# Gelu's upper half by a type-changing DMA within SBUF in four of sixteen slices

## The chip, the cores and the metric

The kernel runs on one core of a Trainium2 chip. Its time is the device time of one execution in microseconds, as the median of several runs. The engines are named as the profile names them: PE (TensorE, with its weight loads as PEld), DVE (VectorE), ACT (ScalarE), POOL (GpSimd) and SP (SyncE).

## The reference

Two stages in float32. First, for each of 4 batches, 49 agents attend to 12480 keys, and then the 12480 queries attend to the agents (width 128). The result, 49920 rows of 128, goes through a feed-forward layer with 2048 hidden values and gelu in its sigmoid form.

```python
def sm(a, b):
    s = scale * (a @ b.transpose(0, 2, 1))
    e = np.exp(s - s.max(-1, keepdims=True))
    return e / (e.sum(-1, keepdims=True) + 1e-09)
agent_v = sm(agents, k) @ v
x = sm(q, agents) @ agent_v
h = x @ w_in
out = (h * (1.0 / (1.0 + np.exp(-1.702 * h)))) @ w_out
```

## The kernel before

**Two parts for a value.** The large matmuls take float32r operands. A value is held as an upper part (a copy to float32r) and a lower part (the value less the upper part). So gelu's result g has the tiles gh (upper) and gl = g - gh (lower), and the products with the weights are summed: upper by upper, lower by upper, upper by lower.

**Groups and slices.** The queries of a batch make 13 groups of 960, so there are 52 groups. Each group goes through the 2048 hidden values in 16 slices f of 128. `up` (L357) makes a slice: four matmuls into two PSUM tiles ph (L362, L364), two gelu on ACT into g (L369), then gh by ACT for even f (`HI_ON_ACT`, L371) or by DVE for odd f (L373), then gl by a subtraction on DVE (L374). `down` (L377) adds a slice to the output with six matmuls (L385): two with gh, two with gl, two with gh again. `down` of a slice is called LAG = 4 slices after its `up`. After a group's last `down`, `store` (L393) copies the sums out and SP stores them.

**Work beside the slices.** For each group, `split` (L165) prepares the queries two groups ahead on POOL: a small memset (L167) and two subtractions (L168, L169) into a tile `rest`, of which there are two. At f = 4 the scores of the next group's queries are made (`scores`, L172): PE writes two PSUM tiles ps_m in turn, of which there are only two, and DVE reduces each (L189); softmax and the transposes for the next group (L345, then L350 to L353 at f = 12) follow. In groups 0 to 5 of a batch (1 to 5 of the first), the keys of the next batch are worked on: two or three blocks in a group, each with a split on POOL at f = 0, 4 (and 8), and scores on PE at f = 5, 9 (and 13), which use the same two ps_m tiles. After the last of them `key_max` (L229) takes the maximum over the batch with two transposes on PE (L235, L241) and copies it to max_b (L242). Then POOL subtracts it from 13 blocks of scores (`key_shift`, L251), and in groups 6 to 11 ACT takes the exponents (L255), ACT and POOL make pairs of them (L260, L261), DVE makes pairs of the values (L267, L268), and PE and DVE add them up (L272, L287). The fourth batch has no such work beside it.

**What sets the order.** The program is written in the order of the loop at L540, and the tile framework's scheduler then places each engine's instructions in an order of its own. Each engine runs its instructions strictly in that order, and an instruction that waits holds back all behind it on its engine. A tile is reused only when its former contents have been read: g has 3 buffers, gh and gl 5 each.

Of the kernel before, what the change touches and what calls it, by code (L numbers as in the profile page):

```python
# [8 lines left out]
F32 = mybir.dt.float32  # L9
F32R = mybir.dt.float32r  # L10
# [7 lines left out]
P = 128  # L18
TB = 120
KB = 8  # L20
CH = 480
GT = 2 * CH
LAG = 4
# [11 lines left out]
K_AT = 5  # L35
FIRST_WORDS = (1, 3, 5, 7)
FIRST_UP = (0, 2, 4, 6)
HI_ON_ACT = (0, 2, 4, 6, 8, 10, 12, 14)
EPS = 1e-09

# [2 lines left out]
def kernel(  # L43
# [10 lines left out]
    nc = tc.nc  # L54
# [14 lines left out]
    gpool = ctx.enter_context(tc.tile_pool(name="gpool", bufs=3))  # L69
# [1 line left out]
    ps_o = ctx.enter_context(tc.tile_pool(name="ps_o", bufs=1, space=bass.MemoryType.PSUM))  # L71
    ps_m = ctx.enter_context(tc.tile_pool(name="ps_m", bufs=2, space=bass.MemoryType.PSUM))

# [1 line left out]
    ag_sb = const.tile([P, B, A], F32, name="ag_sb")  # L75
    nc.sync.dma_start(out=ag_sb, in_=agT)

    ident = const.tile([P, P], F32, name="ident")
    make_identity(nc, ident)
    # sel[k, m] = 1 where k and m name the same agent in either half  # L80
    sel = const.tile([P, P], F32, name="sel")
    nc.vector.memset(sel, 0.0)
    for c in range(2):
        nc.vector.tensor_add(
            out=sel[:, c * H : c * H + A], in0=ident[:, 0:A], in1=ident[:, H : H + A]
# [20 lines left out]
    part_max = const.tile([P, NKG, A], F32, name="part_max")  # L106
    max_b = const.tile([P, A], F32, name="max_b")

    # a float64's words, low then high, to the nearest float32; what is under
    # float32's range becomes zero and what is over it infinite  # L110
    def load_words(src, i):
        w = loads.tile([P, 512, 2], U32, name="words", tag="kv")
        nc.sync.dma_start(out=w.rearrange("p n w -> p (n w)"), in_=src[:, i * 1024 : (i + 1) * 1024])
        return w

    def to_float32(w, out=None):
        lo = w[:, :, 0]
        hi = w[:, :, 1]
        ts = nc.vector.tensor_scalar
        stt = nc.vector.scalar_tensor_tensor  # L120
        # 2 ** exponent, with the sign
        tmp = work.tile([P, 2, 512], U32, name="tmp", tag="rest")
        ex = tmp[:, 0].bitcast(I32)
        ts(out=ex.bitcast(U32), in0=hi, scalar1=20, scalar2=0x7FF, op0=ALU.logical_shift_right, op1=ALU.bitwise_and)
        ts(out=ex, in0=ex, scalar1=1023 - 127, scalar2=1023 + 128, op0=ALU.max, op1=ALU.min)
        ts(out=ex, in0=ex, scalar1=float(127 - 1023), scalar2=float(1 << 23), op0=ALU.add, op1=ALU.mult)
        stt(out=ex.bitcast(U32), in0=hi, scalar=0x80000000, in1=ex.bitcast(U32), op0=ALU.bitwise_and, op1=ALU.bitwise_or)
        # the mantissa's upper 45 bits as a whole number, rounded once
        m = work.tile([P, 512], U32, name="m21", tag="o")
        r = tmp[:, 1]  # L130
        ts(out=m, in0=hi, scalar1=0xFFFFF, scalar2=0x100000, op0=ALU.bitwise_and, op1=ALU.bitwise_or)
        ts(out=r, in0=lo, scalar1=8, scalar2=None, op0=ALU.logical_shift_right)
        stt(out=m.bitcast(F32), in0=m, scalar=float(1 << 24), in1=r, op0=ALU.mult, op1=ALU.add)
        if out is None:
            out = m.bitcast(F32)
        stt(out=out, in0=m.bitcast(F32), scalar=2.0**-44, in1=ex.bitcast(F32), op0=ALU.mult, op1=ALU.mult)
        return out

    def up_weights(i, w):
        to_float32(w, w_in_sb[:, i * 512 : (i + 1) * 512])  # L140

    def down_weights(i, w):
        s = slice(i * 4, (i + 1) * 4)
        wo = to_float32(w).rearrange("p (f c) -> p f c", c=C)
        nc.scalar.copy(out=wo_h[:, s, :], in_=wo)
        nc.vector.tensor_sub(out=wo_l[:, s, :], in0=wo, in1=wo_h[:, s, :].bitcast(F32))

    # ---- scores: a float32 is the sum of three bfloat16, and of the parts'
    # products all are summed but those under a float32 product's own rounding ----
    ag_part = const.tile([P, B, 3, A], BF16, name="ag_part")  # L150
    rest = ag_sb
    for i in range(3):
# [7 lines left out]
        w = t.bitcast(BF16).rearrange("p (n w) -> p n w", w=2)  # L160
        return w[:, :, 1], w[:, :, 0]

    # the upper half of a word is the first part; of what is left the upper
    # half is the second, and the third takes the place of the lower
    def split(t):  # L165
        r = work.tile([P, GT + PAD], F32, name="rest", tag="rest")
        nc.gpsimd.memset(t[:, GT:], 0.0)  # L167
        nc.gpsimd.tensor_sub(out=r, in0=t, in1=halves(t)[0])  # L168
        nc.gpsimd.tensor_sub(out=halves(r)[1], in0=r, in1=halves(r)[0])  # L169
        return halves(t)[0], halves(r)[0], halves(r)[1]  # L170
# [20 lines left out]
                nc.scalar.copy(out=o, in_=s[:, :, 0, :])  # L191
                nc.vector.tensor_add(out=o, in0=s[:, :, 1, :], in1=o)

# [1 line left out]
    def key_load(b, g):  # L195
        t = loads.tile([P, GT + PAD], F32, name="kt", tag="kv")
        nc.sync.dma_start(out=t[:, 0:GT], in_=kT[b, :, g * KB : (g + 1) * KB, :].rearrange("p j t -> p (j t)"))
        return t

    def first_key_scores(g, kt):  # L200
        # two batches' agents to a pass, as many columns as keep the clock up
        for c in range(2):
            ps = ps_m.tile([P, 512], F32, name="ps_m")
            for j in range(KB // 2):
                nc.tensor.matmul(  # L205
                    out=ps[:TB, j * 2 * A : (j + 1) * 2 * A],
                    lhsT=kt[:, c * KB // 2 + j, :],
                    rhs=ag_sb[:, 0:2, :].rearrange("p b a -> p (b a)"),
                    start=True,
                    stop=True,  # L210
                )
            s = ps[:TB, : KB * A].rearrange("p (j b a) -> p j b a", b=2, a=A)[:, :, 0, :]
            i = 2 * g + c
            nc.scalar.copy(out=score[:TB, i * KB // 2 : (i + 1) * KB // 2, :], in_=s)
        nc.vector.tensor_reduce(
            out=part_max[:TB, g, :],
            in_=score[:TB, g * KB : (g + 1) * KB, :].rearrange("p j a -> p a j"),
            axis=AX.X,
            op=ALU.max,
        )  # L220
# [87 lines left out]
            nc.vector.tensor_sub(out=wl[:, s], in0=pw, in1=wh[:, s].bitcast(F32))  # L308
        return wh, wl

# [1 line left out]
    def query_load(b, g):  # L312
        t = loads.tile([P, GT + PAD], F32, name="qt", tag="qt", bufs=2)
        nc.sync.dma_start(out=t[:, 0:GT], in_=qT[b, :, g * GT : (g + 1) * GT])
        return t
# [37 lines left out]
        nc.vector.tensor_sub(out=sb[0:H], in0=ps[H:P, :CH], in1=sb[H:P].bitcast(F32))  # L353
        return sa, sb

# [1 line left out]
    def up(f, wts, pairs):  # L357
        wh, wl = wts
        s = slice(f * P, (f + 1) * P)
        ph = [ps_h.tile([P, 512], F32, name="ph") for _ in range(2)]  # L360
        for c in range(2):
            nc.tensor.matmul(out=ph[c][:, :CH], lhsT=wh[:, s], rhs=pairs[c], start=True, stop=False)  # L362
        for c in range(2):
            nc.tensor.matmul(out=ph[c][:, :CH], lhsT=wl[:, s], rhs=pairs[c], start=False, stop=True)  # L364
        g = gpool.tile([P, 2, CH], F32, name="g")
        gh = gpool.tile([P, 2, CH], F32R, name="gh", bufs=LAG + 1)
        gl = gpool.tile([P, 2, CH], F32R, name="gl", bufs=LAG + 1)
        for c in range(2):
            nc.scalar.activation(out=g[:, c, :], in_=ph[c][:, :CH], func=AF.Gelu_apprx_sigmoid)  # L369
        if f in HI_ON_ACT:  # L370
            nc.scalar.copy(out=gh, in_=g)  # L371
        else:
            nc.vector.tensor_copy(out=gh, in_=g)  # L373
        nc.vector.tensor_sub(out=gl, in0=g, in1=gh.bitcast(F32))  # L374
        return gh, gl
# [21 lines left out]
            t0 = b * N + g * GT + c * CH  # L397
            nc.sync.dma_start(out=outT[:, t0 : t0 + CH], in_=o)

# [1 line left out]
    kts = {}  # L401
    vts = {}
    qts = {}
# [47 lines left out]
    def do_weights(b):  # L451
        wts[b] = agent_weights(accs.pop(b))

    # the first batch's keys and values have nothing to run beside, and lie
    # where the weights and the hidden values come to lie afterwards
    def first_keys():
        tags = [("g", 3), ("gh", LAG + 1), ("gl", LAG + 1)]
        tiles = []
        for tag, bufs in tags:
            tiles += [gpool.tile([P, KB, TB], F32, name="kt0", tag=tag, bufs=bufs) for _ in range(bufs)]  # L460
        return tiles[:NKG]

    for g, t in enumerate(first_keys()):
        nc.sync.dma_start(out=t, in_=kT[0, :, g * KB : (g + 1) * KB, :])
        kts[0, g] = t
# [10 lines left out]
    words = [load_words(w_out, i) for i in range(NF // 4)]  # L476
    for g in range(NKG):
        first_key_scores(g, kts.pop((0, g)))
# [5 lines left out]
    for g in range(NKG):  # L484
# [3 lines left out]
        for j in range(KB):  # L488
            nc.tensor.matmul(
                out=acc_ps[:A, : C + 1],  # L490
# [4 lines left out]
            )  # L495
        if g in FIRST_UP:
            up_weights(FIRST_UP.index(g), words_in[FIRST_UP.index(g)])
        if g == 6:
# [6 lines left out]
    do_weights(0)  # L505
    down_weights(0, words[0])

    # what is done for the next batch beside a group: in steps of the group's
    def beside(b, g):
        jobs = {}  # L510
        if b == 0 and g == 0:
# [25 lines left out]
    steps = B * NG * NF  # L537
    live = {}
    po = {}
    for t in range(steps + LAG):  # L540
        n, f = divmod(t, NF)
        if t < steps:
            b, g = divmod(n, NG)
# [19 lines left out]
        if t >= LAG:  # L563
            n, f = divmod(t - LAG, NF)
# [43 lines left out]
```

## Time and profile before

| | us |
|---|---|
| median of three runs | 2137.14 |
| the three runs | 2136.03, 2137.14, 2139.71 |
| the profiled execution (first to last instruction, its span) | 2139.6 |
| PE busy | 2083.2 (97%) |
| DVE busy | 1865.0 (87%) |
| ACT busy | 1611.9 (75%) |
| POOL busy | 519.8 (24%) |

The profile shows one execution. The page gives no time of it beside the span, so the span stands for its time. Rows of groups give the line, engine and operation, the tiles out<-in, the count, then busy time and mean length, and the idle time before with what ended it. Rows of the timeline begin with start and length in us; a bracket at the end is the engine's idle time before the row and what released it.

### The profile page before, as it was taken

The page shows a single profiled execution, that of the slowest core. Times are in us where ns is not written, and L with a number is a line of the kernel's source. Part 1 is how long each engine was busy: PE and PEld are TensorE (multiplying, and loading weights), DVE is VectorE, ACT ScalarE, POOL GpSimd, SP SyncE. Part 2 cuts the span into 40 slices and gives each one's busy share as a digit, 9 for nine tenths or more (in the row PEclk, how much of TensorE's full clock was granted, in tenths as well). Part 3 has the DMA queues.
Part 4 walks back from the last instruction along what each step waited for, and adds up shares of the span by engine and source line. Part 5 has one row for each costly group of instructions (what it writes and reads, how often), then busy time and mean ns, then how long its engine had stood idle before and what let it go on. Part 6 is the DMA issues. An engine that isn't in the chain of part 4 may idle for free.

```text
span 2139.6 us, 31613 instructions
## 1 busy us (share of the span) xinstructions
PE 2083.2 (97%) x12232; PEld 1777.1 (83%) x12232; DVE 1865.0 (87%) x2142; ACT 1611.9 (75%) x2590; POOL 519.8 (24%) x383
## 2 busy tenths in 40 slices
PE   8889989999999999999999999999999999999999
PEld 8678878888888887788888888778888888888887
DVE  6998998999889899899888899899898887888876
ACT  3567768977777776987777777798777877778786
POOL 4143445121123433421113342531110101001000
PEclk9999999999999999999999999999999999999999
DMA  9411221211111212112101212111100101010000
GB/s 265 119 48 49 65 73 38 61 48 50 38 38 47 66 47 56 47 56 56 56 20 47 63 49 56 55 51 53 47 19 19 38 19 38 19 38 20 25 14 19
DMA packets 49339, 108.57 MB, mean 51 GB/s; under 512 B 4252, under 2 KB 30172, under 8 KB 49188
## 3 DMA queue, kind: packets, MB, share of 16 engines
q1 hardware_dynamic: 49188, 106.55, 17.2%
q8 instruction: 96, 1.57, 0.3%
q14 instruction: 55, 0.45, 0.1%
HBM read 80.97 MB, written 25.56 MB: 50 GB/s over the span
## 4 chain that ended last, share of the span: by engine, by line
PE 81%; DVE 11%; issue 3%; ACT 3%; POOL 1%; DMA 1%; ACTq 0%; SPq 0%; DVEq 0%; POOLq 0%
PE po L385 43%; PE ph L362 15%; PE ph L364 14%; DVE gl L374 5%; DVE gh L373 2%; PE ps_m L272 1%; PE ps_m L182 1%; PE ps_m L184 1%; POOL score L251 1%; PE ps_m L205 1%; ACT g L369 1%; PE ps_m L345 1%; PE ps_m L306 1%; PE ps_m L183 1%; PE ps_m L185 1%
## 5 line engine op out<-in xcount | busy, mean ns | idle before, releaser
L374 DVE TENSOR_TENSOR gl<-g,gh 128x960 fp32r<-128x960 f32 x832 | 1034.4, 1258 | 189.4 <-ACT gh L371 174.3
L369 ACT ACTIVATE g<-ph 128x480 f32<-128x480 f32 x1664 | 855.2, 573 | 380.5 <-PE ph L364 265.7
L385 PE MATMUL po<-gl,wo_h 128*128 128x480 f32 x1664 | 501.9, 382 | 5.4 <-DVE gl L374 5.4
L385 PE MATMUL po<-gh,wo_h 128*128 128x480 f32 x1664 | 506.1, 383 | 0.7 <-ACT gh L371 0.7
L385 PE MATMUL po<-gh,wo_l 128*128 128x480 f32 x1664 | 501.6, 383 | 0.0
L371 ACT CAST gh<-g 128x960 fp32r<-128x960 f32 x416 | 416.0, 1000 | 10.9
L385 PEld LDWEIGHTS po<-gl,wo_h 128*128 128x128 f32 x1664 | 313.1, 189 | 60.0 <-DVE gl L374 9.2
L385 PEld LDWEIGHTS po<-gh,wo_h 128*128 128x128 f32 x1664 | 313.5, 189 | 53.2 <-ACT gh L371 1.1
L385 PEld LDWEIGHTS po<-gh,wo_l 128*128 128x128 f32 x1664 | 313.8, 189 | 49.9
L362 PE MATMUL ph<-sa,wh 128*128 128x480 f32 x832 | 332.5, 400 | 4.8 <-ACT g L369 4.8
L364 PE MATMUL ph<-sa,wl 128*128 128x480 f32 x832 | 319.3, 384 | 0.0
L362 PE MATMUL ph<-sb,wh 128*128 128x480 f32 x832 | 318.8, 383 | 0.0
L364 PE MATMUL ph<-sb,wl 128*128 128x480 f32 x832 | 316.6, 381 | 0.0
L373 DVE CAST gh<-g 128x960 fp32r<-128x960 f32 x416 | 298.6, 718 | 7.0 <-ACT g L369 6.6
L167 POOL MEMSET qt<- 128x8 f32 x52 | 5.7, 110 | 939.2 <-PE ps_m L185 472.0
L169 POOL TENSOR_TENSOR rest<-rest 128x968 bf16<-128x968 f32 x91 | 188.6, 2072 | 7.1
L362 PEld LDWEIGHTS ph<-sa,wh 128*128 128x128 f32 x832 | 157.7, 190 | 31.7 <-ACT g L369 10.8
L362 PEld LDWEIGHTS ph<-sb,wh 128*128 128x128 f32 x832 | 158.0, 190 | 26.6 <-ACT g L369 6.2
L364 PEld LDWEIGHTS ph<-sb,wl 128*128 128x128 f32 x832 | 156.9, 189 | 25.6 <-issue 1.0
L364 PEld LDWEIGHTS ph<-sa,wl 128*128 128x128 f32 x832 | 157.1, 189 | 24.7 <-issue 1.0
L168 POOL TENSOR_TENSOR rest<-qt 128x968 f32<-128x968 f32 x52 | 110.7, 2129 | 167.8 <-DMA qt<-qT 110.8
L184 PE MATMUL ps_m<-ag_part,rest 128*128 128x98 bf16 x728 | 110.2, 205 | 0.0
(103 smaller groups left out, 2077.8 us busy)
## 6 DMA issues: line engine op xcount, KB each, us to landing
kt<-kT SPq DMA_DIRECT2D x52, 480.0 KB, 3.6
qt<-qT SPq DMA_DIRECT2D x52, 480.0 KB, 3.8
vt<-v SPq DMA_DIRECT2D x52, 480.0 KB, 4.3
outT<-o SPq DMA_DIRECT2D x104, 240.0 KB, 2.2
words<-w_in SPq DMA_DIRECT2D x4, 512.0 KB, 10.9
words<-w_out SPq DMA_DIRECT2D x4, 512.0 KB, 8.2
ag_sb<-agT SPq DMA_DIRECT2D x1, 98.0 KB, 2.1
```

Source lines behind the costliest of these rows:

```text
L168: nc.gpsimd.tensor_sub(out=r, in0=t, in1=halves(t)[0])
L169: nc.gpsimd.tensor_sub(out=halves(r)[1], in0=r, in1=halves(r)[0])
L182: mm(out=o, lhsT=x0[:, t], rhs=a[:, 0 : 2 * A], start=True, stop=False)
L183: mm(out=o[:, A:], lhsT=x0[:, t], rhs=a[:, 2 * A :], start=False, stop=False)
L184: mm(out=o, lhsT=x1[:, t], rhs=a[:, 0 : 2 * A], start=False, stop=False)
L362: nc.tensor.matmul(out=ph[c][:, :CH], lhsT=wh[:, s], rhs=pairs[c], start=True, stop=False)
L364: nc.tensor.matmul(out=ph[c][:, :CH], lhsT=wl[:, s], rhs=pairs[c], start=False, stop=True)
L369: nc.scalar.activation(out=g[:, c, :], in_=ph[c][:, :CH], func=AF.Gelu_apprx_sigmoid)
L371: nc.scalar.copy(out=gh, in_=g)
L373: nc.vector.tensor_copy(out=gh, in_=g)
L374: nc.vector.tensor_sub(out=gl, in0=g, in1=gh.bitcast(F32))
L385: nc.tensor.matmul(out=po[c][:, :CH], lhsT=lhsT[:, f, :], rhs=rhs[:, c, :], start=(f == 0 and first), stop=(f == NF - 1 and last),)
```

## The change

In slices 1, 5, 9 and 13 of every group gh is no longer made by a DVE cast but by a DMA from g to gh, both in SBUF, issued on POOL's queue; it changes the type from float32 to float32r. DVE's subtraction for gl is still there and now waits for the DMA. g gets four buffers (three before), gl four (five before). The tiles in which the first batch's keys lie are the same buffers and are counted anew (still 13).

```diff
+HI_ON_DMA = (1, 5, 9, 13)
 HI_ON_ACT = (0, 2, 4, 6, 8, 10, 12, 14)
...
-        g = gpool.tile([P, 2, CH], F32, name="g")
+        g = gpool.tile([P, 2, CH], F32, name="g", bufs=LAG)
         gh = gpool.tile([P, 2, CH], F32R, name="gh", bufs=LAG + 1)
-        gl = gpool.tile([P, 2, CH], F32R, name="gl", bufs=LAG + 1)
+        gl = gpool.tile([P, 2, CH], F32R, name="gl", bufs=LAG)
         for c in range(2):
             nc.scalar.activation(out=g[:, c, :], in_=ph[c][:, :CH], func=AF.Gelu_apprx_sigmoid)
-        if f in HI_ON_ACT:
+        if f in HI_ON_DMA:
+            nc.gpsimd.dma_start(out=gh, in_=g)
+        elif f in HI_ON_ACT:
             nc.scalar.copy(out=gh, in_=g)
         else:
             nc.vector.tensor_copy(out=gh, in_=g)
...
-        tags = [("g", 3), ("gh", LAG + 1), ("gl", LAG + 1)]
+        tags = [("g", LAG), ("gh", LAG + 1), ("gl", LAG)]
```

In the changed kernel's own numbering, lines after the new constant stand one further down, and those after `up` three (L168 becomes L169, L373 becomes L376, L374 becomes L377, L385 becomes L388); the DMA is L372. The text uses the numbers of before unless an order of the changed kernel is shown.

On POOL, in a group with keys beside it (batch 1, its fifth group): rest is the tile of a split, kt and qt are a block of keys and the queries of a group. Before:

```order
L168 TENSOR_TENSOR rest_8383<-kt_8253 128x968
L169 TENSOR_TENSOR rest_8383<-rest_8383 128x968
L167 MEMSET kt_8714 128x8
L168 TENSOR_TENSOR rest_8596<-qt_8245 128x968
L169 TENSOR_TENSOR rest_8596<-rest_8596 128x968
L168 TENSOR_TENSOR rest_8710<-kt_8708 128x968
L169 TENSOR_TENSOR rest_8710<-rest_8710 128x968
```

And now:

```order
L169 TENSOR_TENSOR rest_8383<-kt_8253 128x968
L170 TENSOR_TENSOR rest_8383<-rest_8383 128x968
L168 MEMSET kt_8714 128x8
L169 TENSOR_TENSOR rest_8596<-qt_8245 128x968
L170 TENSOR_TENSOR rest_8596<-rest_8596 128x968
L372 DMA gh_8452<-g_8451 128x960
L169 TENSOR_TENSOR rest_8710<-kt_8708 128x968
L170 TENSOR_TENSOR rest_8710<-rest_8710 128x968
L372 DMA gh_8565<-g_8564 128x960
L372 DMA gh_8656<-g_8655 128x960
```

The DMA of slice 5 (gh_8452) stands behind two splits, that of slice 9 (gh_8565) behind the next group's first split, and that of slice 13 (gh_8656) behind nothing else.

On DVE, in the same group, from the subtraction of slice 1 (gl_8282) to the reduces of the query scores (sd from two ps_m tiles). Before:

```order
L373 CAST gh_8281<-g_8280 128x960
L374 TENSOR_TENSOR gl_8282<-g_8280,gh_8281 128x960
L374 TENSOR_TENSOR gl_8301<-g_8299,gh_8300 128x960
L373 CAST gh_8319<-g_8318 128x960
L374 TENSOR_TENSOR gl_8320<-g_8318,gh_8319 128x960
L189 TENSOR_REDUCE sd_8337<-ps_m_8338 120x196
L189 TENSOR_REDUCE sd_8337<-ps_m_8356 120x196
```

And now:

```order
L377 TENSOR_TENSOR gl_8282<-g_8280,gh_8281 128x960
L377 TENSOR_TENSOR gl_8301<-g_8299,gh_8300 128x960
L376 CAST gh_8319<-g_8318 128x960
L190 TENSOR_REDUCE sd_8337<-ps_m_8338 120x196
L377 TENSOR_TENSOR gl_8320<-g_8318,gh_8319 128x960
L190 TENSOR_REDUCE sd_8337<-ps_m_8356 120x196
```

The cast of slice 1 is gone; the subtraction that needs its DMA is still the first of these rows, and both reduces stand behind it.

On POOL again, where the batch's maximum has been taken (score is the scores, max_b the maximum, gh_9117 slice 13 of that group, gh_9215 slice 1 of the next). Before:

```order
L168 TENSOR_TENSOR rest_9470<-qt_9178 128x968
L169 TENSOR_TENSOR rest_9470<-rest_9470 128x968
L251 TENSOR_TENSOR score_105<-score_105,max_b_107 120x392 x13
L167 MEMSET qt_9606 128x8
L261 TENSOR_TENSOR e_pair0_90<-score_105,e_pair0_90 120x8x49
```

And now:

```order
L169 TENSOR_TENSOR rest_9470<-qt_9178 128x968
L170 TENSOR_TENSOR rest_9470<-rest_9470 128x968
L372 DMA gh_9026<-g_9025 128x960
L372 DMA gh_9117<-g_9116 128x960
L252 TENSOR_TENSOR score_105<-score_105,max_b_107 120x392 x13
L372 DMA gh_9215<-g_9214 128x960
```

The 13 shifts stand together as before, and slice 1's DMA stands behind all of them. On DVE the copy to max_b stood behind the subtraction of slice 14 and still does; the two steps before it (L237, L239) have moved ahead of slice 13's subtraction.

## Prediction

> **What bounds the kernel now.** I read the page's busy table first, then the windows, then the timeline of a group without side work, of one with keys beside it, and of the place where a batch's maximum is taken. The busy table:
>
> ```profile
> PE 2083.2 (97%) x12232; PEld 1777.1 (83%) x12232; DVE 1865.0 (87%) x2142; ACT 1611.9 (75%) x2590; POOL 519.8 (24%) x383
> ```
>
> The windows tell where PE is not full (columns: window, length, then busy us with counts for PE, PEld, DVE, ACT, POOL):
>
> ```profile
> 100.00:200.00 100.00, 91.97 (x622) 76.62 (x622) 94.81 (x106) 66.57 (x109) 41.91 (x27) 0.98 0.18 55
> 200.00:300.00 100.00, 95.38 (x651) 81.63 (x650) 91.57 (x98) 72.51 (x115) 38.54 (x24) 1.00 0.22 65
> 800.00:900.00 100.00, 94.06 (x536) 79.14 (x534) 92.09 (x101) 76.67 (x120) 41.05 (x27) 0.97 0.19 50
> 1000.00:1100.00 100.00, 100.00 (x538) 86.59 (x537) 87.69 (x102) 75.40 (x123) 11.81 (x12) 1.00 0.13 40
> 1300.00:1400.00 100.00, 95.57 (x623) 81.26 (x622) 93.24 (x102) 74.90 (x119) 53.11 (x33) 0.98 0.22 60
> 1400.00:1500.00 100.00, 97.79 (x522) 83.12 (x521) 93.14 (x107) 86.33 (x137) 17.31 (x13) 1.00 0.20 55
> 1900.00:2000.00 100.00, 100.00 (x543) 85.54 (x543) 81.35 (x92) 78.71 (x127) 7.75 (x7) 1.00 0.09 30
> ```
>
> PE is the bound almost everywhere; it has gaps only near the start and around 850 and 1350 us, where DVE is above 90%. All PE idle time is 2139.6 - 2083.2 = 56.4 us. So work taken from DVE can only win inside those few gaps, and anything that makes PE wait elsewhere is lost in full.
>
> A steady stretch shows what a slice costs and how early its values are:
>
> ```profile
> 1216.52 0.38 PE L362 MATMUL ph<-sa,wh 128*128 128x480 f32 x1
> 1217.37 1.03 ACT L369 ACTIVATE g<-ph 128x480 f32<-128x480 f32 x2
> 1218.43 0.66 DVE L373 CAST gh<-g 128x960 fp32r<-128x960 f32 x1
> 1218.70 0.38 PE L362 MATMUL ph<-sa,wh 128*128 128x480 f32 x1
> 1219.13 1.16 DVE L374 TENSOR_TENSOR gl<-g,gh 128x960 fp32r<-128x960 f32 x1
> ```
>
> A slice is 1218.70 - 1216.52 = 2.18 us of PE: ten matmuls 0.218 apart, four up and six down. g is ready 1.88 us after its slice starts (1217.37 + 1.03 = 1218.40). The slice's down matmuls run four slices later, behind that slice's four up matmuls (0.87 us), and take gh first and gl two matmuls (0.44 us) later. So gl is due 8.72 + 0.87 + 0.44 = 10.03 us after the slice starts, and of that 8.15 us lie after g. Less gl's own 1.16 us, a gh that takes up to 6.99 us is hidden, if nothing stands in its way.
>
> **The change, part by part.** Let W be the time from the moment POOL can issue the DMA until gh has landed.
>
> *Removed:* 4 of 8 casts of L373 in each of 52 groups.
>
> ```profile
> L373 DVE CAST gh<-g 128x960 fp32r<-128x960 f32 x416 | 298.6, 718 | 7.0 <-ACT g L369 6.6
> ACT g L369 <- DVE gl L374: 92.3, 74, 2.8
> ```
>
> 208 x 0.718 = 149 us of DVE, 2.87 us a group. Nearly all of it lies beside a full PE. It counts only in the groups with gaps: six near the start, and two each around 850 and 1350. Ten groups x 2.87 = 29 us at most, nothing at least. A fourth buffer of g also shortens ACT's waits for gl (92.3 us), which end in the same gaps. I take half: **-15 us**. gl goes from five buffers to four: gl(f+4) is written after up(f+4) and ACT's 1.03 us, when gl(f) has just been read (0.87 us after that up), so I cost it at nothing; a late PE would make DVE wait there, and nothing then waits for DVE.
>
> *Added: W.* The trace has no DMA from POOL, none within SBUF and none that changes a type. The nearest rows are loads of the same 480 KB in the same 128 rows, issued by SP:
>
> ```profile
> kt<-kT SPq DMA_DIRECT2D x52, 480.0 KB, 3.6
> qt<-qT SPq DMA_DIRECT2D x52, 480.0 KB, 3.8
> ```
>
> No reason makes POOL's faster, so 3.6 us is the low end. Writing the transfer's list in software and converting each value can each cost something; I bound both together by one more such transfer: 7.6 us. I take 3.8 + 1.0 = **4.8 us**, near the row it resembles. By the Trainium skill (DMA: Bandwidth & Descriptors, Anatomy of one DMA) a DMA from POOL takes about 2.0 us plus its bytes at 436 GB/s, 3.1 us here, and its table gives about 1 us to the first byte; an estimate from that page is W = 4.1 us and 2166 us in all by the sum below. No run shown here has such a DMA.
>
> In 35 of 52 groups 4.8 is under 6.99 and POOL is nearly idle: **0 us**.
>
> *Groups with keys (17: five, six and six).* Here DVE waits in its own order, and POOL's splits stand ahead of two of the four DMAs. One such group of before:
>
> ```profile
> 1296.59 0.66 DVE L373 CAST gh<-g 128x960 fp32r<-128x960 f32 x1
> 1302.84 1.04 DVE L189 TENSOR_REDUCE sd<-ps_m 120x196 f32<-120x392 f32 x2
> 1304.62 0.22 PE L182 MATMUL ps_m<-ag_part,kt 128*128 128x98 bf16 x1
> 1305.77 0.46 PE L362 MATMUL ph<-sa,wh 128*128 128x480 f32 x1
> 1306.74 2.67 POOL L168 TENSOR_TENSOR rest<-qt 128x968 f32<-128x968 f32 x1
> 1309.48 1.80 POOL L169 TENSOR_TENSOR rest<-rest 128x968 bf16<-128x968 f32 x1
> 1315.96 2.44 POOL L168 TENSOR_TENSOR rest<-kt 128x968 f32<-128x968 f32 x1 [4.67 <-PE ps_m L185]
> 1318.49 2.60 POOL L169 TENSOR_TENSOR rest<-rest 128x968 bf16<-128x968 f32 x1
> ```
>
> 1296.59 is slice 1's cast. Now DVE stands at gl(1) until 1296.59 + W, and behind it stand gl(2), gh(3), the first reduce of the query scores, gl(3) and the second: 3 x 1.16 for gl(1), gl(2) and gl(3), 0.66, 2 x 0.51 after the wait, so the second reduce is done at 1301.7 + W. The key scores at 1304.62 write those same two PSUM tiles, the second one 0.58 us in (half of their 1.15 us), at 1305.20. PE waits W - 3.45 = 1.35 us.
>
> Slice 5's DMA now stands behind two splits. The second ends at 1311.28; g(5) is there at 1305.77 + 1.88 = 1307.65. PE wants gl(5) at 1305.77 + 8.72 + 1.15 (slice 9's key scores) + 1.31 = 1316.95. From 1311.28 with W and 1.16 that holds to W = 4.5, and the 1.35 us that PE has just lost, less the 0.6 by which they delay the split, move it to 5.2: nothing at 4.8.
>
> Slice 9's DMA stands behind the next group's first split, which waits until slice 9's key scores let its buffer go and ends at 1321.09. Slice 9's up begins with it, near 1315.9; gl(9) is due 10.03 later, at 1325.95, and with 1.16 for gl the room is 3.7 us. PE waits W - 3.70 = 1.1 us.
>
> Together 2.45 us x 17 = **+42 us** (at W = 3.6: 3 us; at 7.6: 4.15 + 3.9 = 8.05, so 137 us).
>
> *The batch's maximum (three times).* POOL's order now has all 13 shifts ahead of slice 1's DMA of the next group.
>
> ```profile
> 844.72 1.94 ACT L369 ACTIVATE g<-ph 128x480 f32<-128x480 f32 x4
> 850.50 0.30 PE L241 MATMUL ps_m<-ident,mrow 49*120 49x49 f32 x1 [3.42 <-DVE mrow L239]
> 850.73 1.17 PE L385 MATMUL po<-gh,wo_h 128*128 128x480 f32 x2
> 853.30 0.60 PE L362 MATMUL ph<-sa,wh 128*128 128x480 f32 x1
> 853.70 0.60 PE L362 MATMUL ph<-sb,wh 128*128 128x480 f32 x1
> 856.22 0.60 PE L385 MATMUL po<-gh,wo_l 128*128 128x480 f32 x2
> 856.66 0.38 PE L362 MATMUL ph<-sa,wh 128*128 128x480 f32 x1
> 851.35 0.19 DVE L242 COPY max_b<-ps_m 120x49 f32<-120x49 f32 x1
> 851.62 16.83 POOL L251 TENSOR_TENSOR score<-score,max_b 120x392 f32<-120x392 f32 x13 [14.65 <-DVE max_b L242]
> 860.46 2.43 ACT L369 ACTIVATE g<-ph 128x480 f32<-128x480 f32 x5
> 867.49 0.59 PE L385 MATMUL po<-gh,wo_h 128*128 128x480 f32 x2
> 875.89 0.48 PE L362 MATMUL ph<-sa,wh 128*128 128x480 f32 x1 [1.60 <-ACT g L369]
> ```
>
> The first row is slices 12 and 13, so slice 13's g is there at 844.72 + 1.94 = 846.66. The copy to max_b now stands behind gl(13), which waits for its DMA, and gl(14): 846.66 + W + 2 x 1.16 + 0.19 = 849.2 + W. The shifts follow 0.27 later and end at 866.3 + W; then slice 1's DMA goes, whose g was there by 860.46 + 1.03 = 861.5, and lands at 866.3 + 2W = 875.9. PE wants that gh at 867.49: 8.4 us of waiting, and 0.7 more for gl (1.16 - 0.44). The mrow wait of 3.42 us gets shorter, since gh(13) and gl(13) are no longer ahead of it, but PE then only waits longer here. The wait of 1.60 us before 875.89 falls into the new one. Right after the wait at 850.50 matmuls began 0.40 us apart instead of 0.22 (853.30, 853.70), until about 856.2: from 850.73 fourteen matmuls took 5.5 us instead of 3.1, so a wait of this length costs 2.4 us more. 8.4 + 0.7 - 1.6 + 2.4 = 9.9, x 3 = **+30 us** (each us of W moves it by 2: at W = 3.6 7.5 x 3 = 22, at 7.6 15.5 x 3 = 46).
>
> *Sum.* -15 + 0 + 42 + 30 = +57 us on this execution's 2139.6, so 2196.6. The three runs have a median of 2137.14, 2.4 us less: **2194 us**.
>
> A rule that speaks against the change: by the Trainium skill (SBUF — State Buffer, Who interferes with whom) a DVE copy or cast in its fast mode holds the port through which POOL writes such a DMA's list. The casts that stay would be such work; with one of 0.718 us in the way each time, W is 5.5 and the sum about 2221. No run shown here tells.
>
> **Rivals.**
>
> *Faster.* DVE's 2.87 us a group and the fourth g close all the gaps. In nine of the 100-us windows, from the row at 100 to the row at 1400 above, PE is not full and lacks 33 us in all, and the DMA is as quick as a load. -33 + 3 + 22 = -8: 2129 us. For it: the rows of them above have DVE at 91.6 to 94.8%. Against it: the shifts' place in POOL's order, which costs 22 us even at 3.6. It decides below a W of about 3.7, and only if nearly all gaps close. 0.20.
>
> *The DMA is long (W near 7).* Changing the type, or writing the list, may double it. Key groups 17 x (3.55 + 3.30) = 116, maxima 3 x 14.3 = 43. 116 + 43 - 15 = +144: 2281 us. At 7.6 the 35 quiet groups lose as well: a late gl moves the next due time too, so one DMA in two waits, 35 x 2 x 0.61 = 43, and with 137 + 46 and no gain 2363 us. For it: no row of the trace has this kind of DMA. Against it: the plain load is half as long. 0.20.
>
> *No change.* W near 3.6 and the gaps half closed: 3 + 22 - 15 = +10, and a little more gain makes it nothing: 2140 us. 0.12.
>
> That gh would still pass DVE is excluded by its order: L376 stands there four times a group instead of eight.
>
> **The numbers.** The forecast (slower, W between 4 and 6) has 0.48; with the long DMA, slower has 0.68; faster 0.20; within 0.2%, about what a measurement of this kernel can tell from no change (4 us), 0.12. The time is that of the forecast. Range: W's low end with all the gain, -29 + 3 + 22, gives 2133; the faster rival reaches 2129 and the range 2126, a little under it. The long DMA is taken in up to 2320, which leaves about 1 in 10 on either side. The forecast's own range is 2162 (W = 4) to 2241 (W = 6).
>
> **What would show it.** In the profile after: DVE's L376 at 208 casts; the landing time of gh<-g (4 to 6 us); in windows over 1650 PE still full and a slice 2.18 us; gl waiting for the DMA as DVE's largest wait; PE's score matmuls waiting for DVE's reduces and down matmuls waiting for slice 9's gl in groups with keys; after each maximum a wait of some 8 us at a down matmul that a DMA behind L252 ends. I am wrong if W is under 3.7 or over 7, if PE has no new wait at the maxima, or if PE's new waits lie in the quiet groups.

## The result and the profile after

The changed kernel takes 2192.98 us (median of 4 runs, 2186.93 to 2199.02) against 2136.68 for the one before beside it (4 runs): a ratio of 1.0258, 95% interval 1.0237 to 1.0278, so slower. The profiled execution has a span of 2190.9 us, 51.3 more than the 2139.6 of before. The prediction said 2194. The number is right, by luck; the rest of this text is on how little of the way to it was.

The page of the kernel after, busy table, groups and the DMA's landing (median us from issue to landing), then three waits (us in total, times, longest):

```profile
PE 2101.1 (96%) x12232; PEld 1785.1 (81%) x12232; DVE 1733.0 (79%) x1934; ACT 1613.8 (74%) x2590; POOL 622.6 (28%) x591
L377 DVE TENSOR_TENSOR gl<-g,gh 128x960 fp32r<-128x960 f32 x832 | 1049.0, 1287 | 292.6 <-DMA gh<-g 145.1 <-ACT gh L374 98.5 <-PE ph L365 12.5
L376 DVE CAST gh<-g 128x960 fp32r<-128x960 f32 x208 | 143.6, 691 | 40.4 <-ACT g L370 40.4
gh<-g POOLq DMA_DIRECT2D x208, 480.0 KB, 2.8
ACT g L370 <- DVE gl L377: 25.2, 12, 6.4
PE ph L363 <- ACT g L370: 16.4, 21, 2.6
PE ps_m L183 <- DVE sd L190: 13.5, 18, 1.9
```

DVE is 132 us less busy, as it should be, with 208 casts left. ACT's waits for gl fell from 92.3 us to 25.2. And PE, the bound, now idles 2190.9 - 2101.1 = 89.8 us (56.4 before), 33.4 us more; the other 17.9 us of the loss lie in its busy time, which is longer for the same 12232 matmuls. Its waits for ACT's g rose from 4.8 us (6 times) to 16.4 (21 times), those for the reduces into sd from 4.5 (twice) to 13.5 (18 times). Four windows, with the columns of those before:

```profile
200.00:300.00 100.00, 92.93 (x635) 78.24 (x634) 83.75 (x90) 67.28 (x109) 40.54 (x32) 1.00 0.31 99
800.00:900.00 100.00, 91.20 (x591) 75.05 (x590) 82.09 (x85) 70.06 (x112) 52.50 (x41) 0.98 0.33 104
1000.00:1100.00 100.00, 100.00 (x558) 86.52 (x557) 82.93 (x93) 78.18 (x126) 21.89 (x26) 1.00 0.32 104
1900.00:2000.00 100.00, 97.36 (x495) 82.82 (x494) 71.66 (x78) 75.90 (x123) 16.03 (x19) 0.98 0.21 75
```

DVE went down by 5 to 10 points, and PE did not go up in any of them. To place the loss I cut both timelines at ACT's copy into sa, which stands once in each group; the stretch from the n-th copy to the next is called group n. Group 17, a group with keys, runs from 722.31 to 761.39 before (39.08 us) and from 745.07 to 785.89 after (40.82):

```profile
722.31 0.56 ACT L350 CAST sa<-ps_m 64x480 fp32r<-64x480 f32 x1 [0.91 <-PE ps_m L345]
761.39 0.56 ACT L350 CAST sa<-ps_m 64x480 fp32r<-64x480 f32 x1 [0.90 <-PE ps_m L345]
```

```profile
745.07 0.55 ACT L351 CAST sa<-ps_m 64x480 fp32r<-64x480 f32 x1 [1.01 <-PE ps_m L346]
785.89 0.55 ACT L351 CAST sa<-ps_m 64x480 fp32r<-64x480 f32 x1 [0.95 <-PE ps_m L346]
```

Done so for every group, and with the experiments beside it (us more than before, from the profiled executions; "rest" is what lies ahead of the first such copy). The key scores of the first batch lie in groups 2 to 6, those of the others in 14 to 19 and 27 to 32:

| groups | after | buffers alone | slice 1 alone | without slice 1 | order alone | query's chain first |
|---|---|---|---|---|---|---|
| the first, no keys | +2.4 | +1.8 | +2.1 | -8.5 | +1.1 | +5.1 |
| 17 with keys | +29.9 | +1.4 | +38.1 | +13.6 | +23.3 | +10.4 |
| 6 at and behind the maxima | +12.1 | -4.6 | +1.5 | -3.3 | +5.0 | +8.8 |
| 15 quiet, batches 1 to 3 | -0.5 | -0.3 | +0.2 | +5.9 | +1.2 | +9.2 |
| batch 4 | +5.3 | -0.1 | +2.6 | +6.2 | -0.3 | +5.2 |
| rest | +2.2 | -0.4 | +1.3 | +0.6 | +1.9 | -0.2 |
| sum | +51.4 | -2.1 | +45.8 | +14.6 | +32.3 | +38.4 |

Nine of the 17 groups with keys lose 1.69 to 1.95 us; the others lie between -3.5 and +4.1. One of the nine is group 17. Of its 1.74 us PE idles 1.26, and its busy time is the rest longer (39.56 us against 39.08). First DVE and POOL before, and then DVE after (start, length, idle time before the row):

```profile
740.05 1.16 DVE L374 TENSOR_TENSOR gl<-g,gh 128x960 fp32r<-128x960 f32 x1
741.24 1.04 DVE L189 TENSOR_REDUCE sd<-ps_m 120x196 f32<-120x392 f32 x2
742.31 0.56 DVE L321 TENSOR_REDUCE m<-sd 120x8 f32<-120x392 f32 x1
742.90 0.57 DVE L322 TENSOR_TENSOR sd<-sd,m 120x392 f32<-120x392 f32 x1
743.79 2.35 DVE L374 TENSOR_TENSOR gl<-g,gh 128x960 fp32r<-128x960 f32 x1 [0.32 <-ACT gh L371]
741.01 1.86 POOL L168 TENSOR_TENSOR rest<-kt 128x968 f32<-128x968 f32 x1
742.94 2.19 POOL L169 TENSOR_TENSOR rest<-rest 128x968 bf16<-128x968 f32 x1
```

```profile
760.90 2.23 DVE L377 TENSOR_TENSOR gl<-g,gh 128x960 fp32r<-128x960 f32 x2 [3.18 <-DMA gh<-g]
763.04 0.65 DVE L376 CAST gh<-g 128x960 fp32r<-128x960 f32 x1
763.73 0.57 DVE L190 TENSOR_REDUCE sd<-ps_m 120x196 f32<-120x392 f32 x1
764.21 2.37 DVE L377 TENSOR_TENSOR gl<-g,gh 128x960 fp32r<-128x960 f32 x1
766.50 0.55 DVE L190 TENSOR_REDUCE sd<-ps_m 120x196 f32<-120x392 f32 x1
767.09 0.56 DVE L322 TENSOR_REDUCE m<-sd 120x8 f32<-120x392 f32 x1
767.57 1.68 DVE L377 TENSOR_TENSOR gl<-g,gh 128x960 fp32r<-128x960 f32 x1
769.18 2.16 DVE L323 TENSOR_TENSOR sd<-sd,m 120x392 f32<-120x392 f32 x1
```

The wait for the DMA (3.18 us) is there. But DVE reaches the first reduce of the query scores 18.66 us after the copy into sa (763.73 - 745.07), against 18.93 before: it is not late. It becomes late behind that reduce: gl(3), which stood ahead of both reduces, now stands between them, and gl(4), which stood behind the scores' subtraction, ahead of it. They now begin while rows of POOL's split run and take 2.37 and 1.68 us; the scores' subtraction does so too and takes 2.16 instead of 0.57. It ends 26.27 us after the copy, against 21.16 before. The split, in POOL's rows after:

```profile
763.77 1.80 POOL L169 TENSOR_TENSOR rest<-kt 128x968 f32<-128x968 f32 x1
765.64 2.60 POOL L170 TENSOR_TENSOR rest<-rest 128x968 bf16<-128x968 f32 x1
768.24 2.67 POOL L169 TENSOR_TENSOR rest<-qt 128x968 f32<-128x968 f32 x1
```

The rows end in step: gl(3) at 766.58, 1.01 us after POOL's row from 763.77; gl(4) at 769.25, 1.01 us after the row from 765.64; the scores' subtraction at 771.34, 0.43 us after the row from 768.24. So each waits until the POOL row at hand is done. Before, the split ran beside these rows as well, but the subtraction began at 742.90, in the gap between two of POOL's rows, and took 0.57.

What waits for DVE: the key scores for the second reduce, then ACT, which has loaded the table for exp (now behind the first half of slice 5's gelu, with the second half held back), and so PE (two rows of ACT and two of PE after):

```profile
769.19 1.28 ACT L329 ACT_TABLE_LOAD   x1
771.37 0.53 ACT L329 ACTIVATE sd<-sd 120x392 f32<-120x392 f32 x1 [0.90 <-DVE sd L323]
```

```profile
767.11 0.20 PE L183 MATMUL ps_m<-ag_part,kt 128*128 128x98 bf16 x1 [0.58 <-DVE sd L190]
773.84 0.48 PE L363 MATMUL ph<-sb,wh 128*128 128x480 f32 x1 [0.67 <-ACT g L370]
```

At the first maximum POOL's 13 shifts stand ahead of slice 1's DMA, as foreseen (POOL, then PE):

```profile
340.32 14.55 POOL L252 TENSOR_TENSOR score<-score,max_b 120x392 f32<-120x392 f32 x13 [6.35 <-DVE max_b L243]
354.82 0.57 POOL L372 DMA_DIRECT2D gh<-g  x1
```

```profile
358.75 1.17 PE L388 MATMUL po<-gh,wo_h 128*128 128x480 f32 x2 [4.18 <-DMA gh<-g]
361.11 1.17 PE L388 MATMUL po<-gl,wo_h 128*128 128x480 f32 x2 [1.19 <-DVE gl L377]
```

### The profile page after: what moved, and what is told of

Read it like the earlier page. It is cut to its first block, busy times and chain, and to the rows that moved or that the text cites. A ratio compares the mean times of both kernels' runs of the same rounds, so it can differ in the third digit from the quotient of the medians.

```text
span 2190.9 us, 32087 instructions
## 1 busy us (share of the span) xinstructions
PE 2101.1 (96%) x12232; PEld 1785.1 (81%) x12232; DVE 1733.0 (79%) x1934; ACT 1613.8 (74%) x2590; POOL 622.6 (28%) x591
## 4 chain that ended last, share of the span: by engine, by line
PE 73%; DVE 13%; ACT 5%; issue 4%; DMA 2%; POOL 2%; ACTq 0%; DVEq 0%; SPq 0%; POOLq 0%
PE po L388 40%; PE ph L363 14%; PE ph L365 13%; DVE gl L377 7%; ACT g L370 2%; DVE sd L323 2%; POOL score L252 2%; DMA gh<-g 1%; PE ps_m L273 1%; ACT L370 1%; PE ps_m L206 1%; PE ps_m L346 1%; ACT gh L374 1%; DVE sd L190 1%; DVE gh L376 1%
## 5 line engine op out<-in xcount | busy, mean ns | idle before, releaser
L377 DVE TENSOR_TENSOR gl<-g,gh 128x960 fp32r<-128x960 f32 x832 | 1049.0, 1287 | 292.6 <-DMA gh<-g 145.1
L388 PE MATMUL po<-gh,wo_h 128*128 128x480 f32 x1664 | 506.0, 385 | 11.2 <-DMA gh<-g 10.5
L388 PE MATMUL po<-gl,wo_h 128*128 128x480 f32 x1664 | 506.2, 385 | 10.5 <-DVE gl L377 10.5
L388 PE MATMUL po<-gh,wo_l 128*128 128x480 f32 x1664 | 506.6, 385 | 0.0
L374 ACT CAST gh<-g 128x960 fp32r<-128x960 f32 x416 | 416.6, 1001 | 10.0
L388 PEld LDWEIGHTS po<-gl,wo_h 128*128 128x128 f32 x1664 | 314.8, 190 | 66.7 <-DVE gl L377 16.0
L388 PEld LDWEIGHTS po<-gh,wo_h 128*128 128x128 f32 x1664 | 314.0, 189 | 65.8 <-DMA gh<-g 12.4
L372 POOL DMA_DIRECT2D gh<-g x208 | 115.3, 554 | 878.7 <-ACT g L370 725.3
L388 PEld LDWEIGHTS po<-gh,wo_l 128*128 128x128 f32 x1664 | 316.1, 190 | 51.8 <-issue 1.4
L170 POOL TENSOR_TENSOR rest<-rest 128x968 bf16<-128x968 f32 x91 | 199.4, 2191 | 5.6
L376 DVE CAST gh<-g 128x960 fp32r<-128x960 f32 x208 | 143.6, 691 | 40.4 <-ACT g L370 40.4
L169 POOL TENSOR_TENSOR rest<-qt 128x968 f32<-128x968 f32 x52 | 110.6, 2127 | 153.2 <-DMA qt<-qT 72.7
```

What stands on the lines that cost most here:

```text
L372: nc.gpsimd.dma_start(out=gh, in_=g)
L388: nc.tensor.matmul(out=po[c][:, :CH], lhsT=lhsT[:, f, :], rhs=rhs[:, c, :], start=(f == 0 and first), stop=(f == NF - 1 and last),)
```

## The experiments

The theories at the start. A: the DMA of slice 1 costs, by what it does around the query scores on DVE, and the shifts ahead of it at the maxima. B, the prediction's: each DMA's length costs, in slice 9 behind a split as well as in slice 1. Times before are of the same chip.

**The buffers alone.**

```diff
-HI_ON_DMA = (1, 5, 9, 13)
+HI_ON_DMA = ()
```

> The new buffer counts alone (g four, gl four), no slice by DMA: every upper part is made by ACT or DVE as before. Both theories: the cost is the DMA's, so 2130 to 2140 us against 2137; the fourth g can only shorten ACT's waits for gl (92 us before). If instead the four buffers of gl hold DVE back, 2150 us or more.

2136.6 us against 2139.94, ratio 0.9984 (0.9974 to 0.9993). The fourth buffer of g in place of gl's fifth costs nothing and gains about 3 us, as expected of the buffers by both theories. Among all kernels here it is the quickest, and by a hair quicker than the one before.

**One slice, and the other three.**

```diff
-HI_ON_DMA = (1, 5, 9, 13)
+HI_ON_DMA = (1,)
```

> Only slice 1 of each group by DMA. Theory A (what costs is the wait for slice 1's DMA ahead of the query scores on DVE, with the order that it brings there, and the shifts ahead of slice 1's DMA at the maxima): nearly all of the loss stays, 2175 to 2190 us. Theory B (the prediction's: each DMA's length counts, and slice 9's behind a split costs nearly half of a key group's loss): about half stays, 2160 to 2170 us.

2187.51 us, 1.0223 (1.0208 to 1.0239), in A's range and far from B's: slice 1 alone loses 47.6 us against the kernel before on its chip, where all four lose 56.3.

```diff
-HI_ON_DMA = (1, 5, 9, 13)
+HI_ON_DMA = (5, 9, 13)
```

> Slices 5, 9 and 13 by DMA, slice 1 by DVE again. Theory A: the loss is gone, 2125 to 2142 us, and PE has no wait at the key scores. Theory B: slice 9 goes on costing 1.1 us in 17 key groups, 2150 to 2165 us.

2155.58 us, 1.0074 (1.0057 to 1.0090). The number lies in B's range and outside A's, but the place is not B's: of the six plus six key groups of the second and third round eight lose nothing (-0.01 to 0.04 us), though the DMAs of slices 5 and 9 are still issued late there, behind splits (1.7 and 3.0 us after their g in group 17). So at this landing time the splits ahead of a DMA cost nothing, which rules out B's slice 9. What remains is scattered: the first two groups shift against each other (-8.5 and +10.4), and quiet groups and the last batch lose 12 us. Of these 12, 7 lie in eight groups in which a single transfer lands late (3.4 to 5.3 us after its issue); the rest is open.

**Slice 1 of the group behind the maximum on DVE again.**

```diff
-        if f in HI_ON_DMA:
+        if by_dma:
...
-            live[t] = up(f, wts[b], pairs[n])
+            live[t] = up(f, wts[b], pairs[n], f in HI_ON_DMA and not (b + 1 < B and g == 6 and f == 1))
```

> As the changed kernel, but slice 1 of the three groups that follow a maximum is cast on DVE, so that no DMA stands behind the 13 shifts. If the shifts hold back that DMA and PE with it, each of the three places gets 4 to 8 us shorter, 2168 to 2182 us. If PE's wait there only moves to another cause (the shifts, ACT's tables), 2188 to 2196 us.

2181.85 us, 1.0197 (1.0179 to 1.0216), at the upper end of the first range: 9 us less than the changed kernel by the spans (2182.1 against 2190.9), 11 by the medians and 14 by what each loses against the kernel before on its own chip. The six groups at and behind the maxima lose 8.6 us less (12.1 to 3.5), the three with the shifts in them 2.5 to 4.8 each, not the 4 to 8 that were expected, while the key groups lose some 1.76 us as before. So the shifts ahead of slice 1's DMA are a cause, worth 9 to 14 us.

**DVE's order without any DMA.** The question left was why slice 1 costs 1.76 us in a group with keys: the wait for its DMA, or the order in which the scheduler has put DVE's work since. Here nothing is on a DMA, and the order of the changed kernel is forced: gl(3) is issued behind the first reduce (r), and the scores' subtraction (shift) behind gl(4).

```diff
-HI_ON_DMA = (1, 5, 9, 13)
+HI_ON_DMA = ()
...
+                while between:
+                    done["low"] = between.pop(0)(r.ins)
...
+            shift(*[low(top).ins for low in held])
```

> No slice is on a DMA, the buffers are the changed kernel's, and VectorE's order around the query scores is made to be the changed kernel's: first reduce, gl(3), second reduce, maximum, gl(4), subtraction (the one before has both reduces, the maximum and the subtraction with no subtraction of a gl between the reduces). Theory order: what costs 1.7 us in each group with keys is that two subtractions of gl (about 1.2 us each, 2.4 beside a split on POOL) have come to stand ahead of the second reduce and of the scores' subtraction; then 17 such groups lose about as much here too: 2155 to 2170 us. Theory lateness: it is the 3.2 us for which gl(1) waits for its DMA, with all of VectorE behind it; there is none here: 2135 to 2145.

2171.74 us, 1.0144 (1.0127 to 1.0162). That is just above the range. Of the 12 key groups of the second and third round 8 lose 1.71 to 1.79 us, the very amount. Its group 17, the copy into sa, then DVE, ACT and PE:

```profile
734.24 0.55 ACT L362 CAST sa<-ps_m 64x480 fp32r<-64x480 f32 x1 [0.91 <-PE ps_m L357]
```

```profile
752.32 0.57 DVE L190 TENSOR_REDUCE sd<-ps_m 120x196 f32<-120x392 f32 x1 [0.38 <-PE ps_m L186]
754.47 0.56 DVE L329 TENSOR_REDUCE m<-sd 120x8 f32<-120x392 f32 x1
755.73 2.79 DVE L390 TENSOR_TENSOR gl<-g,gh 128x960 fp32r<-128x960 f32 x1 [0.70 <-PE ps_m L186]
758.43 2.16 DVE L333 TENSOR_TENSOR sd<-sd,m 120x392 f32<-120x392 f32 x1
```

```profile
760.62 0.53 ACT L340 ACTIVATE sd<-sd 120x392 f32<-120x392 f32 x1 [1.72 <-DVE sd L333]
```

```profile
763.09 0.49 PE L374 MATMUL ph<-sb,wh 128*128 128x480 f32 x1 [1.49 <-ACT g L381]
```

No DMA, and DVE is even early at the reduces; gl(4) begins beside a row of the split and takes 2.79 us, the subtraction ends 26.35 us after the copy into sa (26.27 in the changed kernel), and PE waits for ACT in the same place, 1.49 us. Theory "lateness" falls: the order alone is enough. ACT's order moved with DVE's here, and the two were not tried apart.

**The other way round: all DMAs, the query's chain first.**

```diff
-        nc.vector.tensor_sub(out=gl, in0=g, in1=gh.bitcast(F32))
+        def low(after):
+            with tc.issue_after(after):
+                return nc.vector.tensor_sub(out=gl, in0=g, in1=gh.bitcast(F32))
...
+            if f == Q_AT:
+                while held:
+                    held.pop(0)(done["sub"].ins)
```

> The changed kernel, all four slices on DMAs, with both reduces, the maximum and the subtraction of the query scores put on VectorE ahead of gl(3) and gl(4). Theory order: the groups with keys (17, 1.7 us each) lose nothing now and the wait at the maxima stays: 2155 to 2170 us. Theory lateness: gl(1) waits as before and the reduces behind it come late all the same: 2185 to 2195. Half of each would be 2172 to 2182.

2180.59 us, 1.0196 (1.0182 to 1.0210), between the two ranges. By place it is clear: five key groups that lost 1.76 to 1.82 us now lose 0.45 to 0.66 (14, 16, 17, 18 and 27); where these 0.45 to 0.66 lie was not followed up. In its group 17, again the copy into sa and then DVE, the subtraction takes 0.59 us and ends 20.92 us after the copy:

```profile
735.30 0.56 ACT L351 CAST sa<-ps_m 64x480 fp32r<-64x480 f32 x1 [1.36 <-PE ps_m L346]
```

```profile
753.96 1.04 DVE L190 TENSOR_REDUCE sd<-ps_m 120x196 f32<-120x392 f32 x2
755.63 0.59 DVE L323 TENSOR_TENSOR sd<-sd,m 120x392 f32<-120x392 f32 x1
```

But held back in every group, gl(3) and gl(4) now come late where there are no keys: the 15 quiet groups lose 9.2 us, 2.0 in the first of each batch.

**That order in key groups alone, and the maxima mended.**

```diff
+ by_dma = f in HI_ON_DMA and not (b + 1 < B and g == 6 and f == 1)
...
+ live[t] = up(f, wts[b], pairs[n], by_dma, held if f in (Q_AT - 1, Q_AT) and b + 1 < B and g < 6 else None)
```

> The changed kernel with two things undone, all DMAs but three kept: in groups with keys the query's reduces, maximum and subtraction stand ahead of gl(3) and gl(4), and slice 1 of the three groups after the key maximum is cast on VectorE. If these two are the cost: 17 groups get back 1.3 us each (22) and the maxima 11, so 2155 to 2165. If there is a third cost that both hide: over 2170.

2158.07 us, 1.0079 (1.0061 to 1.0098), inside the range. Two causes give back 35 of the 56 us, with 205 of 208 DMAs still there. Left on its span are 17 us: 5.3 in key groups (0.42 to 0.52 us in seven of them, more or less in others), 4.8 in the first group, 2.5 at the maxima, 5.2 in one group of the last batch.

**DMAs only in groups without keys, maximum or shifts.**

```diff
-            live[t] = up(f, wts[b], pairs[n])
+            live[t] = up(f, wts[b], pairs[n], f in HI_ON_DMA and (b + 1 == B or 8 <= g <= 11))
```

> The four slices go to DMAs only in the groups that have no keys, no maximum and no shifts beside them: groups 8 to 11 of the first three batches and all 14 of the last, 26 of 52. Theory: there the DMA is hidden, as the prediction has it at anything up to 6.99 us, and what is left is the kernel with the buffers alone: 2135 to 2140 us. Rival: single transfers that land late (a tenth take 3.4 to 6.5 us from issue to landing) cost 0.3 us a group or more on the mean: 2143 to 2150.

2140.75 us, 1.0011 (0.9999 to 1.0023), just above the theory's range: no difference to be measured from before, 4 us behind the buffers alone by the medians and 6 against the kernels before. The groups are 25, not 26. The DMA is hidden for the most part; where the few us come from was not followed up.

**DMAs only at the maxima.**

```diff
-            live[t] = up(f, wts[b], pairs[n])
+            live[t] = up(f, wts[b], pairs[n], f in HI_ON_DMA[1:] and b + 1 < B and g in (5, 6))
```

> Slices 5, 9 and 13 go to DMAs only in groups 5 and 6 of the first three batches, those of the key maximum and behind it; slice 1 stays on VectorE everywhere. Theory: VectorE's relief shortens the wait for the maximum (2 to 4 us at each of three): 2128 to 2134 us, faster than both kernels. Rival: the buffers alone have brought what there is: 2135 to 2138.

2138.1 us, 1.0002 (0.9993 to 1.0010). I was wrong here: relief for DVE where it is busiest gains nothing beyond the buffers. So in no place tried does this DMA win anything in this kernel.

**A plain copy, one of four issued by SP.**

```diff
-            nc.gpsimd.dma_start(out=gh, in_=g)
+            (nc.sync if f == 9 else nc.gpsimd).dma_start(out=gh.bitcast(F32), in_=g)
```

> The changed kernel with the four DMAs as plain copies of the same type, and that of slice 9 issued by SP; the order on VectorE is the changed kernel's. The upper part isn't rounded then and the lower part is zero in these slices. Theory order: what the DMA does to the type and who issues it has no part in the cost: each landing within 0.5 us of 2.8, time 2180 to 2200. Rival, the change of type or POOL's issue is what a DMA costs: 2140 to 2165.

2201.45 us, 1.0277 (1.0247 to 1.0307), just above the first range and far from the second. The landings:

```profile
gh<-g POOLq DMA_DIRECT2D x156, 480.0 KB, 2.8
gh<-g SPq DMA_DIRECT2D x52, 480.0 KB, 3.0
```

The change of type costs nothing that shows, and SP is no quicker an issuer.

**A later DMA.**

```diff
-            nc.gpsimd.dma_start(out=gh, in_=g)
+            nc.gpsimd.tensor_copy(out=idle[:, 0:8], in_=g[:, 1, 0:8])
+            for _ in range(4):
+                last = nc.gpsimd.memset(idle, 0.0)
+            with tc.issue_after(last.ins):
+                nc.gpsimd.dma_start(out=gh, in_=g)
...
```

> The changed kernel with VectorE's order around the query scores held as it has it, and with about 1 to 2 us of idle work on POOL (a tiny copy of g, then four memsets) between g and each issue, so that gh lands some 4.2 to 5.2 us after g, near the 4.8 that the prediction took. Theory that the prediction's formulas hold and only their size was off: each group with keys loses (W - 3.45) + (W - 3.70) more, 2.45 us at 4.8, 17 of them 42 us, and the three maxima 10 more: 2230 to 2260. Rival, the groups have more room than that: 2193 to 2210. In groups without keys both expect nothing up to 6.99.

DVE's order around the query scores is held by the code of the order experiment, left out here. 2443.94 us, 1.1418 (1.1383 to 1.1453): far outside both ranges. The added work was longer than meant (2.7 us), so gh landed 6.3 us after g in the median (5.3 at least), and 17 groups with keys lost 126 us (the formulas give 17 x (2.85 + 2.6) = 93), the first group 9, the six at the maxima 38, the 15 quiet ones 81 and the last batch 48.

```profile
DVE gl L398 <- DMA gh<-g: 352.6, 165, 9.1
ACT g L382 <- DVE gl L398: 182.3, 85, 6.7
PEld po L411 <- DMA gh<-g: 136.4, 51, 6.4
PE po L411 <- DMA gh<-g: 115.6, 48, 6.0
```

At 6.3 us nothing is hidden, not in quiet groups either: DVE waits 352.6 us, ACT behind it for buffers of g, PE for both. PE's own rows grew too (busy 2192.9 us against 2101.1, mean granted clock 0.952 against 0.986). The scheduler also moved casts and splits about in this kernel, so how much of it is the transfer's time alone stays open.

## Why the prediction was right and wrong, point by point

**W: wrong.** The step "No reason makes POOL's faster, so 3.6 us is the low end" failed. Loads come from outside SBUF and this DMA does not, though whether that is the reason was not tried; it lands 2.84 us after its issue (median of 208, least 2.77) and 3.16 after g is there. 4.8 was 1.6 too long. The estimate from the Trainium skill (DMA: Bandwidth & Descriptors, Anatomy of one DMA), 4.1 us, was nearer but still 0.9 above; that section's formula alone gives 3.1, close to the trace, and what made it 4.1 was the 1 us to the first byte that the prediction added. The rule of the Trainium skill on a DVE cast that keeps POOL from writing a DMA's list (SBUF — State Buffer, Who interferes with whom) would have made W 5.5 us if a cast were in the way each time; by the trace 182 of 208 landings lie within 0.22 us of the least, so W is not 5.5. Only 17 of the 208 issues had a DVE cast beside them, and 14 of these had other traffic beside them too, so the rule itself is hardly tested here.

**Relief of DVE, -15 us: wrong.** It bought nothing where it was tried apart: buffers alone gain 3 us, and DMAs at the maxima add nothing to that. The six groups at the start, on which I had counted, did not get shorter but are 5.0 us longer, in which the cost of the new order is included; they were not tried apart.

**Quiet groups, 0 us: right** at this W (-0.5 us in 15 groups, and no loss over 0.3 us in 11 of the last batch's 13). The room that I gave it, 6.99 us, isn't borne out: with a W of 6.3 us they lost 81 us, though the order had moved there too.

**Groups with keys, +42 us: right in sign and not far off in size (+29.9), wrong in cause.** At the measured W both formulas, W - 3.45 and W - 3.70, give nothing. The first step that failed: "3 x 1.16 for gl(1), gl(2) and gl(3)", durations of a quiet stretch; gl(3) waits out a row of the split and took 2.37, and so the second reduce ended 6.15 us after the wait instead of 5.16. With these 0.99 us the first formula gives W - 2.46 = 0.70, near the 0.58 that PE waits there in group 17. The second: the sum ended at that reduce. Behind it stood the maximum, gl(4), the subtraction and exp, and the working never asked how gl(4) stood to the subtraction. The order of DVE was shown ahead of the prediction as far as the second reduce; the next three rows would have shown it. The experiments settle this: that order alone, without any DMA, costs the 1.77 us, and undoing it with the DMAs in place gives 1.1 to 1.4 of them back in five groups; the rest stays open. That slice 9's DMA waits behind a split costs nothing at this W.

**Maxima, +30 us: right in cause, too large.** The shifts do hold back slice 1's DMA, PE's wait of 4.18 and 1.19 us is where it was foreseen, and taking it away gives back 9 to 14 us for three. With a W of 3.16 the formula would have had 9.9 - 3.3 = 6.6 us each, 20 in all. The groups at and behind the three maxima lost 7.9, 1.7 and 2.5 us, 12.1 in all, and 16.7 more than with the buffers alone.

**In all:** with the measured W the prediction's own sum is -15 + 0 + 0 + 20 = +5, about no change. It came to +57 because a DMA taken too long stood in for an order that was not followed: that the sum met the measured loss is luck. Of the rivals, "no change" came nearest in W and fell by the same omission.

## What to carry to other kernels

When a change takes an instruction out of an engine's queue, read the whole new order up to the last instruction that another engine waits for: a scheduler fills the hole, and what it moves can cost more than what was moved off. Take an instruction's duration from the stretch where it will run, and ask what the other engine has in hand when it begins (here 1.16 or 2.4 us for the same subtraction). An engine at 87% that isn't the bound need not have anything to give; here relieving it of 132 us gained nothing, and none of the five placements of the DMA came out below the buffers alone.

## What the runs showed of the hardware

A DMA of 480 KB within SBUF that changes the type lands in 2.84 us, one that doesn't in about the same (2.8 from POOL, 3.0 from SP), both sooner than a load (3.6 to 4.2), and its landing is very even: of 208, the 148 with neither a load's or store's packet nor an instruction fetch beside them took 2.99 us at most. All 22 that took over 3.2 us had one of these beside them, but so had 34 that took 2.99 at most. The slowest one of the last batch, in the stretch from its issue to its landing:

```profile
q0 software_dynamic: 144, 0.49, 26.7%
q8 instruction: 1, 0.02, 2.2%
gh<-g POOLq DMA_DIRECT2D x1, 480.0 KB, 5.1
```

One packet of instructions had 2.2% of 16 engines for 5.3 us, which is 1.9 us of one engine, about what this landing is longer than the others. The group lost 4.6 us, nearly all that the last batch lost. That they fall together is counted; that the one causes the other was not tried.

A subtraction on DVE waits for POOL: in the profile after, each of the 106 subtractions into gl that began while one of POOL's tensor-tensor rows ran ended 1.01 to 1.06 us after that row, and so took up to 2.8 us. The other 726 took 1.16 us at most, 44 of them with a row of POOL that began during them. The reduces that began beside such a row took 0.55 to 0.57 us, as elsewhere.
